# Fewer dummy matmuls, 128x32 tiles for the state weights, and a new order of steps in an attention and token-mixer kernel

## The chip, the core and the metric

The kernel runs on one core of one Trainium2 chip. The metric is the device time of one execution in microseconds. The kernel before took 88.55 us, the median of 9 runs that lay between 87.74 and 88.79.

A core has five engines that work side by side and wait for each other by semaphores: TensorE (PE in the profile; its weight loads are shown apart as PEld), VectorE (DVE), ScalarE (ACT), GpSimd (POOL) and SyncE (SP). [...] DMAs are issued here by SP, ACT and POOL.

## The reference

For each of 8 batches and 8 heads there are 512 tokens x of width 64 and 32 states of width 64. The first half reads the states by softmax attention from the tokens (`xread`) and the tokens from the states (`sread`); the second half is a token mixer on the 544 rows of both, with the heads side by side (width 512).

```python
scores  = x @ state.T / 8;        a  = softmax(scores)      # over 32 states
xread   = a @ state
scores2 = state @ x.T / 8;        a2 = softmax(scores2)     # over 512 tokens
sread   = a2 @ x
y   = concat(xread, sread)                    # (8, 544, 512), heads side by side
wq, wk  = y @ w_q, y @ w_k                    # width 64
W_tok   = wq @ wk.T / 8                      # 544 x 544
out = relu(W_tok @ y) @ w_out
```

## The kernel before

The kernel never forms the 544 x 544 matrix. For each batch it forms `wk.T @ y`, which is 64 x 512 (the tile V), and multiplies it by `wq`. It also never forms `xread`: since `xread = a @ state`, the product `xread @ w_q` is `a @ (state @ w_q)`, and `state @ w` (the "state weights", tile `sw`) is computed once for all batches.

All work is cut into named steps. One string, `ORDER`, lists them as `name.batch.mode`; the kernel walks the list and emits the instructions of each step. There is no scheduler behind it: each engine's queue is in the order of the list, and an engine that has to wait holds up all that is behind it in its queue. The pools hand out buffers in the same order. The last letter is the engine or form: `a` ScalarE, `v` VectorE, `p` POOL, `s` a DMA of SP; for TensorE `t` is one matmul of the whole 128x128 array, `c` the same work as two matmuls of 64 columns side by side (128x64 tiles), `r` a form with its own tiling.

The steps of a batch b, in the order of its data:

- `ix`: POOL issues the load of x (512 KB as bf16; POOL's DMA converts from float32). Batch 0 comes by other queues and is cast by `xc`. `iwo` loads w_out, `is` the later states.
- `xT0`, `xT1` (lines 262 to 274, by the helper of lines 165 to 174): TensorE transposes x, heads 0 to 3 and 4 to 7; `xTe` copies the result out of PSUM.
- `pt`, `exp`: scores and their exponentials, the tile E, in two halves.
- `rs`, `rinv`, `A` (lines 330 to 351): row sums of E on VectorE, their reciprocals, and on POOL the normalised tile A. `rs0.b` and `rs1.b` sum one half each, `rs.b` both halves in one instruction.
- `at`, `ate`: A transposed, and copied out (AT).
- `sums`, `srd`, `srn`, `sbd`, `srT`, `srTe`: the attention of the states to the tokens. `srd` is 32 matmuls of 128x32 tiles.
- `wq`, `wks`, `wk`, `g`, `v` and their copies `wqe`, `wke`, `ge`, `ve`: the token mixer's two factors.
- `mix`, `mixs` (64x128 tiles) with `mxe`, `mse`: the mixed rows with the relu (tile rmix).
- `fin`, `oe`, `os`: the product with w_out for 128 tokens at a time. Two such products share a PSUM tile, are copied out together (`oe`) and stored with one DMA of 512 KB (`os`). `fix` and `oc` are the same for 128 tokens alone, with a store of 256 KB issued by ScalarE (mode `a`) or SP. Mode `b` splits the copy and the store of the last piece between two engines. `fs`, `fse` are the rows of the states, four batches at a time.

At the start the states are transposed (`stt`) and copied into the tile stT by `ste` and `stf` (lines 209 to 230): the upper 64 partitions hold the heads of one half, the lower 64 those of the other, and the rest is zero, written by `zst`. `stbd` is a block form of the states that POOL builds. `sw` (lines 241 to 262) multiplies them with w_q and w_k: for two batches, four heads q and two halves r, 16 matmuls of 128 columns.

`fill` (lines 152 to 155) issues dummy matmuls on a tile of zeros, 128 x 512, into a PSUM tile that nobody reads. Eight more, on line 132, stand ahead of everything.

PSUM has two pools: psA with 2 tiles of two banks (`fill`, `sw`, `mix`, `fin`) and psB with 4 tiles of one bank (all else). The pool `tail` holds the single output pieces on their way out.

Of the kernel before, what the change touches and what calls it, by code (L numbers as in the profile page):

```python
# [13 lines left out]


ORDER = """
zst.0.p ix1.0.p stc.0.v xc1.0.a fill.1.t stt.0.c ste.0.v stbd.0.p stf.0.a xc0.0.p xc3.0.v ix2.0.p
fill.7.t xT0.0.t xc2.0.v xTe0.0.a fill.1.t xT1.0.t is.0.p stc.1.v fill.1.t stt.1.c xTe1.0.v stbd.2.p
fill.1.t pt0.0.t stf.1.v fill.1.t pt1.0.t exp0.0.a ste.1.v iwo.0.p exp1.0.a rs0.0.v fill.4.t
sums.0.t ix3.0.p rinv0.0.v wc.0.a fill.1.t xT0.1.t rs1.0.v fill.1.t srd.0.r xTe0.1.v A0.0.p fill.1.t  # L20
xT1.1.t fill.1.t sw.0.r xTe1.1.a rinv1.0.v fill.1.t pt0.1.t srn.0.v A1.0.p at0.0.t srT.0.t exp0.1.a
pt1.1.t srTe.0.v sbd.0.p swe.0.a xT0.2.t rs0.1.v at1.0.t exp1.1.a xT1.2.t xTe0.2.v stbd.1.p ate.0.a
xTe1.2.v fill.1.t stt.2.c stt.3.c rs1.1.v ste.2.a pt0.2.t stbd.6.p stf.3.v exp0.2.a fill.1.t wq.0.c
ste.3.v wks.0.c ix4.0.p stf.2.a wk.0.t rs0.2.v sw.3.r pt1.2.t wke.0.v swe.3.a stbd.3.p sw.1.r
rinv.1.v exp1.2.a g.0.t sw.2.r ge.0.v stbd.5.p swe.1.a rs1.2.v sums.2.t v.0.c wqe.0.a rinv.2.v
xT1.3.c swe.2.a A.1.p ve.0.v xT0.3.c xTe1.3.a srd.2.r xTe0.3.v mix0.0.r mix1.0.r mxe0.0.v sums.1.t
mxe1.0.a A.2.p srd.1.r at.1.t pt1.3.t srn.1.v ate.1.a fin0.0.t srn.2.v ix5.0.p xT1.4.t exp1.3.a
srT.1.t xT0.4.t xTe1.4.v srTe.1.a fin1.0.t sbd.1.p xTe0.4.a rs1.3.v pt1.4.t wq.1.c sbd.2.p exp1.4.a
wks.1.c wqe.1.v pt0.4.t oe0.0.a srT.2.t wk.1.t rs1.4.v at.2.t ix6.0.p fin2.0.t ate.2.v wke.1.a
os0.0.s exp0.4.a stbd.7.p g.1.t srTe.2.v fin3.0.t ge.1.v rs0.4.v sums.4.t stbd.4.p oe1.0.a srd.4.r  # L30
rinv.4.v v.1.c srn.4.v wq.2.c A.4.p ve.1.a os1.0.s srT.4.c wks.2.c wk.2.t srTe.4.a mixs.1.r wke.2.v
mix1.1.r wqe.2.a mix0.1.r mse.1.v xT1.5.t mxe0.1.a ix7.0.p at.4.t xTe1.5.v g.2.t xT0.5.t mxe1.1.a
ge.2.v sbd.4.p pt1.5.t xTe0.5.v v.2.c exp1.5.a fin2.1.c ve.2.v pt0.5.c rs1.5.v mixs.2.r mix1.2.r
exp0.5.a ate.4.v xT1.6.c mse.2.a sums.5.c fin3.1.c xTe1.6.a rs0.5.v rinv.5.v xT0.6.c mxe1.2.a
oe1.1.v A.5.p pt1.6.c wq.4.c srd.5.r exp1.6.a mix0.2.r srn.5.v os1.1.s fin0.1.c mxe0.2.a rs1.6.v
sbd.5.p xT0.7.c xTe0.6.v fin0.2.c xTe0.7.a wqe.4.v pt0.6.c srT.5.c at.5.c exp0.6.a xT1.7.c ate.5.v
srTe.5.a fin1.2.c xTe1.7.a rs0.6.v wq.5.c rinv.6.v wks.5.c wk.5.c wqe.5.a pt1.7.c A.6.p wke.5.v
wks.4.c sums.6.c exp1.7.a srd.6.r g.5.t oe0.2.a rs1.7.v wk.4.t pt0.3.t fin1.1.t srn.6.v exp0.3.a
os0.2.s wke.4.v sbd.6.p at.6.t oe0.1.a rs0.3.v srT.6.t g.4.t fin2.2.t ate.6.v os0.1.s fin3.2.t
ge.5.v ge.4.v srTe.6.v v.5.c oe1.2.a rinv.3.v wq.6.c ve.5.v A.3.p wks.6.c wk.6.c v.4.c os1.2.s  # L40
wke.6.a wqe.6.v mix1.5.r ve.4.a mixs.5.r mix0.5.r mxe1.5.v sums.3.t mxe0.5.a g.6.t srd.3.r mixs.4.r
ge.6.v mix0.4.r mse.5.a mix1.4.r srn.3.v mxe0.4.a v.6.c mse.4.v sbd.3.p srT.3.c pt0.7.c srTe.3.v
at.3.c mxe1.4.a ve.6.v fin2.5.c ate.3.v exp0.7.a fin3.5.c rs0.7.v wq.3.c oe1.5.a wks.3.c fin0.4.c
rinv.7.v A.7.p wqe.3.a os1.5.s mix0.6.r mixs.6.r wk.3.t mse.6.a fin1.4.t wke.3.a mxe0.6.a g.3.t
oe0.4.v at.7.t sums.7.t ate.7.a srd.7.r mix1.6.r srn.7.v os0.4.s fin2.4.c mxe1.6.v sbd.7.p srT.7.c
fin3.4.c srTe.7.a ge.3.v fin2.6.c oe1.4.v v.3.c fin3.6.c ve.3.v os1.4.s fin0.5.c oe1.6.a fin1.5.c
os1.6.s mix1.3.r oe0.5.v mixs.3.r wq.7.c mxe1.3.a wks.7.c wk.7.c mixs.0.r mse.3.v mix0.3.r os0.5.s
mse.0.a wke.7.v fin0.6.c wqe.7.a mxe0.3.a g.7.c fin1.6.c ge.7.a fin0.3.c oe0.6.v fin1.3.c os0.6.s
v.7.c oe0.3.a fin2.3.c ve.7.a fin3.3.c os0.3.s mix0.7.r oe1.3.a mixs.7.r fs.3.t mxe0.7.v mse.7.a
os1.3.s mix1.7.r fse.3.v fs.7.t mxe1.7.a fse.7.v fix1.7.t fix2.7.t oc1.7.a fix0.7.t oc2.7.a fix3.7.t  # L50
oc0.7.a oc3.7.b
"""


# [1 line left out]
def kernel(  # L56
# [20 lines left out]
    NP = H // 2  # L77
# [3 lines left out]

    const = ctx.enter_context(tc.tile_pool(name="const", bufs=1))
    work = ctx.enter_context(tc.tile_pool(name="work", bufs=4))
    tail = ctx.enter_context(tc.tile_pool(name="tail", bufs=7))
    psA = ctx.enter_context(tc.tile_pool(name="psA", bufs=2, space=bass.MemoryType.PSUM))
    psB = ctx.enter_context(tc.tile_pool(name="psB", bufs=4, space=bass.MemoryType.PSUM))

# [4 lines left out]
    stT = const.tile([128, B, 2, H, NS], BF, name="stT")  # L92
    stbd = const.tile([128, B, 2, NP, D], BF, name="stbd")
    w_f = const.tile([128, NP, 2, DH], FP, name="w_f")
    w_qk = const.tile([128, NP, 2, DH], BF, name="w_qk")
    w_o = const.tile([128, KC, DM], BF, name="w_o")
    sw = const.tile([128, B, 2, 2, DH], BF, name="sw")
# [143 lines left out]
    def sw_mm(n, p, e):  # L241
        ps = psA.tile([128, 2, 512], FP, name="sw_ps", tag="psA")
        for bb in range(2):
            for q in range(NP):
                for r in range(2):
                    nc.tensor.matmul(
                        out=ps[NS * q : NS * q + NS, r, 2 * DH * bb : 2 * DH * bb + 2 * DH],
                        lhsT=stT[64 * r : 64 * r + 64, 2 * p + bb, r, NP * r + q, :],
                        rhs=w_qk[64 * r : 64 * r + 64, q, 0:2, :],
                        start=True,  # L250
                        stop=True,
                    )
        G["sw", p] = ps
# [363 lines left out]
    def fs_ev(n, b, e):  # L617
# [7 lines left out]
        "zst": zeros, "stt": st_tr, "ste": st_ev, "stf": st_ev,  # L625
        "stbd": stbd_blk, "fill": fill, "fix": fin_mm, "os": fin_st,
        "sw": sw_mm, "swe": sw_ev, "xT": xT_mm, "xTe": xT_ev, "xs": x_dT, "as": a_dT, "pt": pt_mm, "exp": pt_exp,
        "rs": rs, "rinv": rv, "A": nrm, "at": at_mm, "ate": at_ev,
        "srd": srd, "sums": sums, "srn": srn, "sbd": sbd, "srT": srT_mm, "srTe": srT_ev,
# [38 lines left out]
```

The softmax here doesn't subtract the row's maximum and nothing guards it: scores larger than these inputs give would overflow.

## Time and profile before

| | before |
|---|---|
| median of 9 runs | 88.55 us |
| lowest, highest | 87.74, 88.79 us |
| the profiled execution | 88.63 us |
| its span in the profile | 86.9 us |
| TensorE busy | 80.4 us (93%) |
| VectorE, ScalarE, POOL busy | 52.3, 56.0, 45.1 us |
| last matmul ends | 82.8 us |
| last store landed | 85.9 us |
| output stores: 512 KB, 256 KB, 128 KB pieces | 14, 5, 2 |
| granted TensorE clock | 1.0 |

The profile is of one execution. Its span starts with the first instruction that the profile shows; 1.7 us of the measured time lie outside. Busy time of TensorE is not a measure of how near it is to its peak, since matmuls are pipelined and their ends are modelled; the starts are measured. Some records of matmuls are missing, among them a few of line 155 and 163.

### The profile page before, as it was taken

The page shows a single profiled execution, that of the slowest core. Times are in us where ns is not written, and L with a number is a line of the kernel's source. Part 1 is how long each engine was busy: PE and PEld are TensorE (multiplying, and loading weights), DVE is VectorE, ACT ScalarE, POOL GpSimd, SP SyncE. Part 2 cuts the span into 40 slices and gives each one's busy share as a digit, 9 for nine tenths or more (in the row PEclk, how much of TensorE's full clock was granted, in tenths as well). Part 3 has the DMA queues.
Part 4 walks back from the last instruction along what each step waited for, and adds up shares of the span by engine and source line. Part 5 has one row for each costly group of instructions (what it writes and reads, how often), then busy time and mean ns, then how long its engine had stood idle before and what let it go on. Part 6 is the DMA issues. An engine that isn't in the chain of part 4 may idle for free.

```text
span 86.9 us, 3553 instructions
## 1 busy us (share of the span) xinstructions
PE 80.4 (93%) x1572; PEld 53.2 (61%) x1579; DVE 52.3 (60%) x111; ACT 56.0 (64%) x83; POOL 45.1 (52%) x58
## 2 busy tenths in 40 slices
PE   4999999999999999999899999999999999999910
PEld 1336676868777688777479747866755565544400
DVE  2135993997956867887746957881688264056010
ACT  1543629989888678588597838967930592665530
POOL 7999969999999969308506735327150000000000
PEclk9999999999999999999999999999999999999999
DMA  0899999999709999993600374201461663566782
GB/s 18 284 320 188 207 188 200 193 159 140 100 6 119 154 129 307 294 169 55 245 8 0 145 315 183 104 8 57 185 234 57 274 283 134 213 270 276 292 316 82
DMA packets 15119, 15.00 MB, mean 173 GB/s; under 512 B 3712, under 2 KB 12672, under 8 KB 15104
## 3 DMA queue, kind: packets, MB, share of 16 engines
q0 software_dynamic: 9104, 4.36, 40.7%
q1 hardware_dynamic: 4880, 8.98, 27.9%
q10 hardware_dynamic: 1120, 1.44, 4.6%
q8 instruction: 12, 0.20, 0.9%
q14 instruction: 3, 0.02, 0.1%
HBM read 10.22 MB, written 8.91 MB: 220 GB/s over the span
## 4 chain that ended last, share of the span: by engine, by line
PE 76%; DMA 10%; ACT 4%; DVE 2%; POOL 2%; issue 1%; POOLq 0%
PE fin_ps L161 17%; PE fin_ps L163 11%; DMA x_bf<-in_x_dram 10%; PE fill_ps L155 6%; PE xT_ps L174 4%; PE mix_ps L541 4%; PE warm_ps L132 4%; PE at_ps L174 2%; PE srd_ps L369 2%; PE xT_ps L170 2%; POOL A L346 2%; PE pt_ps L163 2%; PE fins_ps L163 2%; PE v_ps L505 2%; PE g_ps L163 2%; PE wq_ps L433 2%
## 5 line engine op out<-in xcount | busy, mean ns | idle before, releaser
L346 POOL TENSOR_TENSOR A<-E,rinv 128x1024 bf16<-128x1024 bf16 (+1 forms) x9 | 15.4, 1716 | 12.5 <-DVE rinv L340 12.1
L161 PE MATMUL fin_ps<-w_o,rmix 128*64 128x512 bf16 x160 | 19.4, 380 | 0.0
L142 ACT COPY ost<-fin_ps 128x1024 f32<-128x1024 f32 (+2 forms) x13 | 11.2, 864 | 11.6 <-PE fin_ps L161 5.9
L148 ACT ACTIVATE rmix<-mix_ps 128x1024 bf16<-128x1024 f32 x12 | 12.1, 1024 | 2.4 <-PE mix_ps L541 2.4
L407 POOL TENSOR_TENSOR sbd<-srn,mask 128x256 bf16<-128x256 bf16 x16 | 9.4, 613 | 6.0 <-DVE srn L397 5.9
L144 DVE COPY ost<-fin_ps 128x1024 f32<-128x1024 f32 (+1 forms) x6 | 6.5, 1091 | 9.9 <-PE fin_ps L163 5.4
L161 PEld LDWEIGHTS <-rmix 128*64 128x64 bf16 x160 | 8.4, 110 | 6.2 <-issue 0.6
L332 DVE TENSOR_REDUCE rsum<-E 128x16 f32<-128x512 bf16 x16 | 10.8, 676 | 0.8 <-ACT E L317 0.6
L163 PE MATMUL fin_ps<-w_o,rmix 128*128 128x512 bf16 x44 | 11.0, 379 | 0.2
L317 ACT ACTIVATE E<-pt_ps 128x512 bf16<-128x512 f32 x16 | 9.5, 601 | 2.4 <-PE pt_ps L161 1.3
L142 ACT COPY xT<-xT_ps 128x1024 bf16<-128x1024 bf16 x7 | 7.1, 1012 | 4.3 <-PE xT_ps L174 3.1
L234 POOL TENSOR_TENSOR stbd<-st_bf,mask 128x256 bf16<-128x256 bf16 x16 | 9.3, 610 | 0.4 <-DVE st_bf L144 0.4
L144 DVE COPY xT<-xT_ps 128x1024 bf16<-128x1024 bf16 x9 | 6.2, 691 | 2.1 <-PE xT_ps L174 1.9
L155 PE MATMUL fill_ps<-zero 128*128 128x512 bf16 x21 | 7.4, 408 | 0.1
L150 DVE TENSOR_SCALAR rmix<-mix_ps 128x1024 bf16<-128x1024 f32 x4 | 4.9, 1222 | 3.4 <-PE mix_ps L541 3.4
L163 PEld LDWEIGHTS <-rmix 128*128 128x128 bf16 x48 | 4.3, 98 | 4.0 <-ACT rmix L148 0.2
L183 POOL DMA_DIRECT2D x_bf<-in_x_dram x7 | 6.6, 949 | 0.0
L174 PE MATMUL xT_ps<-ident,x_bf 128*128 128x128 bf16 x80 | 6.0, 219 | 0.2 <-ACT E L317 0.2
L174 PEld LDWEIGHTS <-x_bf 128*128 128x128 bf16 x80 | 5.1, 98 | 1.3 <-issue 0.5
L541 PE MATMUL mix_ps<-wq,V 64*128 64x256 bf16 x64 | 5.8, 272 | 0.0
L132 PE MATMUL warm_ps<-zero 128*128 128x512 bf16 x8 | 3.6, 631 | 1.2 <-DVE mask L133 1.2
L144 DVE COPY AT<-at_ps 128x1024 bf16<-128x1024 bf16 x5 | 3.4, 687 | 1.9 <-PE at_ps L170 1.7
(90 smaller groups left out, 140.2 us busy)
## 6 DMA issues: line engine op xcount, KB each, us to landing
out_dram<-ost SPq DMA_DIRECT2D x14, 512.0 KB, 2.7
x_bf<-in_x_dram POOLq DMA_DIRECT2D x7, 512.0 KB, 7.5
out_dram<-ost ACTq DMA_DIRECT2D x3, 256.0 KB, 2.1
x_f<-in_x_dram ACTq DMA_DIRECT2D x2, 256.0 KB, 4.2
x_f<-in_x_dram SPq DMA_DIRECT2D x2, 256.0 KB, 4.6
w_o<-in_moe_w_out_dram POOLq DMA_DIRECT2D x1, 512.0 KB, 8.8
out_dram<-ost SPq DMA_DIRECT2D x2, 256.0 KB, 2.4
st_bf<-in_state_dram POOLq DMA_DIRECT2D x1, 160.0 KB, 7.6
```

The source lines that it names most:

```text
L142: nc.scalar.copy(out=out, in_=in_)
L144: nc.vector.tensor_copy(out=out, in_=in_)
L148: nc.scalar.activation(out=out, in_=in_, func=AF.Relu)
L155: nc.tensor.matmul(out=ps, lhsT=zero[:, 0:128], rhs=zero, start=True, stop=True)
L161: nc.tensor.matmul(out=out[64 * h : 64 * h + 64], lhsT=lh, rhs=rhs, **kw)
L163: nc.tensor.matmul(out=out, lhsT=lhsT, rhs=rhs, **kw)
L174: nc.tensor.transpose(out=out, in_=in_, identity=ident)
L234: nc.gpsimd.tensor_tensor(out=stbd[:, b, r], in0=st_bf[:, b, r : r + 1, :].to_broadcast((128, NP, D)), in1=mask[:, :, None].to_broadcast(( ...
L317: nc.scalar.activation(out=L[b]["E"][:, r].rearrange("p c q n -> p c (q n)"), in_=L[b][f"pt{r}"], func=AF.Exp, scale=float(scale),)
L332: nc.vector.reduce_sum(out=L[b]["rsum"][:, w], in_=L[b]["E"].rearrange("p r c q n -> p (r c q) n")[:, w], axis=AX.X,)
L346: eng.tensor_tensor(out=L[b]["A"].rearrange("p r c q n -> p (r c q) n")[:, w], in0=L[b]["E"].rearrange("p r c q n -> p (r c q) n")[:, w], ...
L407: nc.gpsimd.tensor_tensor(out=L[b]["sbd"][:, r], in0=L[b]["srn"][:, r : r + 1, :].to_broadcast((128, NP, D)), in1=mask[:, :, None].to_broa ...
```

## The change

- `ORDER` is another list. It has 404 steps instead of 410; 19 dummy matmuls in `fill` instead of 23, with two fewer ahead of the first transposes (`fill.5` for `fill.7`), one fewer ahead of `sums.0` (`fill.3` for `fill.4`) and none ahead of `stt.2`.
- The row sums of batches 3 to 7 are one step each (`rs.3.v`) instead of two.
- Eight output pieces of the last batches are made and stored singly: `fix2.5`, `fix3.5`, `fix2.6`, `fix3.6` with their `oc` take the place of `fin2.5` to `fin3.6` with `oe1.5`, `os1.5`, `oe1.6`, `os1.6`; the four of batch 7 were single before. The pool `tail` has 12 buffers instead of 7.
- The matmuls of `sw` read all 128 partitions of stT and of w_qk instead of 64: their weights are 128x32 tiles instead of 64x32.
- Many steps stand elsewhere in the order, and some have another engine or form: for instance `xTe0.0` and `ate.0` go from ScalarE to VectorE, four `xT` steps go from `c` to `t`, batch 3 comes in its turn instead of late, and the loads `ix3` to `ix7` stand behind other work of POOL.

```diff
-    tail = ctx.enter_context(tc.tile_pool(name="tail", bufs=7))
+    tail = ctx.enter_context(tc.tile_pool(name="tail", bufs=12))
...
-                        lhsT=stT[64 * r : 64 * r + 64, 2 * p + bb, r, NP * r + q, :],
-                        rhs=w_qk[64 * r : 64 * r + 64, q, 0:2, :],
+                        lhsT=stT[:, 2 * p + bb, r, NP * r + q, :],
+                        rhs=w_qk[:, q, 0:2, :],
```

Of the list, the first lines, a middle stretch and the last lines (cut):

```diff
 ORDER = """
-zst.0.p ix1.0.p stc.0.v xc1.0.a fill.1.t stt.0.c ste.0.v stbd.0.p stf.0.a xc0.0.p xc3.0.v ix2.0.p
-fill.7.t xT0.0.t xc2.0.v xTe0.0.a fill.1.t xT1.0.t is.0.p stc.1.v fill.1.t stt.1.c xTe1.0.v stbd.2.p
-fill.1.t pt0.0.t stf.1.v fill.1.t pt1.0.t exp0.0.a ste.1.v iwo.0.p exp1.0.a rs0.0.v fill.4.t
-sums.0.t ix3.0.p rinv0.0.v wc.0.a fill.1.t xT0.1.t rs1.0.v fill.1.t srd.0.r xTe0.1.v A0.0.p fill.1.t
-xT1.1.t fill.1.t sw.0.r xTe1.1.a rinv1.0.v fill.1.t pt0.1.t srn.0.v A1.0.p at0.0.t srT.0.t exp0.1.a
+zst.0.p ix1.0.p stc.0.v fill.1.t stt.0.c stbd.0.p xc1.0.a stf.0.v ste.0.a xc0.0.p xc3.0.v ix2.0.p
+fill.5.t xT0.0.t xc2.0.v fill.1.t xT1.0.t xTe0.0.v is.0.p stc.1.v fill.1.t pt0.0.t xTe1.0.v stbd.1.p
+fill.1.t stt.1.c exp0.0.a stf.1.v fill.1.t pt1.0.t rs0.0.v iwo.0.p exp1.0.a rinv0.0.v fill.3.t
+sums.0.t rs1.0.v A0.0.p fill.1.t xT0.1.t wc.0.a rinv1.0.v fill.1.t srd.0.r ste.1.v fill.1.t xT1.1.t
+A1.0.p srn.0.v fill.1.t at0.0.t xTe1.1.a fill.1.t sw.0.r xTe0.1.v fill.1.t srT.0.t ix3.0.p at1.0.t
+srTe.0.v pt0.1.t swe.0.a ate.0.v xT1.2.t pt1.1.t exp0.1.a sbd.0.p xTe1.2.v wq.0.c exp1.1.a wks.0.c
+rs0.1.v stt.3.c stbd.7.p wqe.0.a wk.0.t sums.1.t ste.3.v xT0.2.t wke.0.a stf.3.v pt1.2.t stbd.3.p
+xTe0.2.v srd.1.r exp1.2.a stt.2.c srn.1.v pt0.2.t ste.2.a stbd.4.p g.0.t stf.2.v srT.1.t sw.3.r
+exp0.2.a ge.0.v sw.1.r rs1.1.v v.0.c ix4.0.p swe.1.a rinv.1.v sums.2.t ve.0.a srTe.1.v srd.2.r A.1.p
...
-oe1.1.v A.5.p pt1.6.c wq.4.c srd.5.r exp1.6.a mix0.2.r srn.5.v os1.1.s fin0.1.c mxe0.2.a rs1.6.v
-sbd.5.p xT0.7.c xTe0.6.v fin0.2.c xTe0.7.a wqe.4.v pt0.6.c srT.5.c at.5.c exp0.6.a xT1.7.c ate.5.v
+mxe1.2.v wk.3.t mse.2.a xT1.6.t wke.3.a xT0.6.t xTe1.5.a mxe0.2.v pt1.4.t fin2.1.t exp1.4.a pt1.5.t
+xTe1.6.v fin0.1.t exp1.5.a xTe0.6.v sums.4.t pt1.6.t rs.5.v g.3.t exp1.6.a fin1.1.t ge.3.a fin3.1.t
+rinv.5.v oe0.1.a rs.4.v A.5.p xT0.7.t oe1.1.a fin0.2.t os0.1.s rinv.4.v xTe0.7.v fin1.2.t os1.1.s
...
-v.7.c oe0.3.a fin2.3.c ve.7.a fin3.3.c os0.3.s mix0.7.r oe1.3.a mixs.7.r fs.3.t mxe0.7.v mse.7.a
-os1.3.s mix1.7.r fse.3.v fs.7.t mxe1.7.a fse.7.v fix1.7.t fix2.7.t oc1.7.a fix0.7.t oc2.7.a fix3.7.t
-oc0.7.a oc3.7.b
+mse.6.v mse.5.a mix1.6.r wke.7.v mxe0.6.a fix3.5.c g.7.c mxe1.6.a oc3.5.v fin0.5.c fin1.5.c ge.7.a
+wqe.7.a fin0.6.c oe0.5.a fin1.6.c os0.5.s v.7.c oe0.6.a fix2.5.c ve.7.a fix2.6.c os0.6.s oc2.5.v
+mixs.7.r mix0.7.r oc2.6.v mse.7.a mix1.7.r fix3.6.t mxe1.7.a mxe0.7.v fs.7.t oc3.6.a fix0.7.t
+fse.7.v fix3.7.t oc0.7.a fix2.7.t oc3.7.v fix1.7.t oc2.7.v oc1.7.b
```

POOL's queue, from the two lists (DMA issues in bold):

- before: zst, **ix1**, stbd.0, xc0, **ix2**, **is**, stbd.2, **iwo**, **ix3**, A0.0, A1.0, sbd.0, stbd.1, stbd.6, **ix4**, stbd.3, stbd.5, A.1, A.2, **ix5**, sbd.1, sbd.2, **ix6**, stbd.7, stbd.4, A.4, **ix7**, sbd.4, ...
- after: zst, **ix1**, stbd.0, xc0, **ix2**, **is**, stbd.1, **iwo**, A0.0, A1.0, **ix3**, sbd.0, stbd.7, stbd.3, stbd.4, **ix4**, A.1, stbd.2, **ix5**, A.2, sbd.1, sbd.2, **ix6**, A.3, sbd.3, stbd.5, **ix7**, stbd.6, A.5, ...

## The prediction

> **What bounds the kernel now.** I read the page's busy shares first, then the stretches of time, then the chain of work that ended last, and last the queue of POOL.
>
> ```profile
> span 86.9 us, 3553 instructions
> ...
> PE 80.4 (93%) x1572; PEld 53.2 (61%) x1579; DVE 52.3 (60%) x111; ACT 56.0 (64%) x83; POOL 45.1 (52%) x58
> ...
> 20.00:42.00 22.00, 21.79 (x545) 16.66 (x546) 17.16 (x36) 17.91 (x27) 17.25 (x21) 1.00 0.96 157
> 42.00:83.00 41.00, 40.28 (x738) 25.33 (x741) 22.95 (x43) 26.08 (x38) 9.85 (x10) 1.00 0.43 171
> ```
>
> The columns of the last two lines are the stretch, its length, and the busy time of PE, PEld, DVE, ACT and POOL. TensorE has no free time from 20 to 83 us; every other engine has. The chain says what lies between its steps:
>
> ```profile
> 5.56 1.89 PE fill_ps L155 x7
> 9.44 0.23 PE pt_ps L163 x8
> 14.23 0.60 ACT E L317
> 14.88 0.61 PE xT_ps L174 x8
> 17.66 0.50 ACT E L317
> 18.20 0.32 PE wk_ps L459 x8
> 18.86 0.23 PE sw_ps L246 x16
> 19.09 0.34 PE pt_ps L163 x8
> 33.31 8.87 DMA x_bf<-in_x_dram
> 42.18 0.04 issue
> 42.22 0.64 PE xT_ps L170 x16
> ```
>
> Columns: start, length, what. Three things are to be seen. The same eight pt matmuls take 0.23 us behind a fill and 0.34 behind sw: 0.11 us belongs to the change of tile shape. TensorE waits in three places: at 14.88 and 18.20 for ACT, at 42.22 for a load of x. In the single starts of the trace these waits are 0.34, 0.30 and 0.49 us, 1.13 together. And a load of x takes up to 8.87 us from issue to landing. POOL issues these loads between its other work:
>
> ```profile
> 27.50 0.94 POOL L183 DMA_DIRECT2D x_bf<-in_x_dram  x1
> 28.46 2.32 POOL L234 TENSOR_TENSOR stbd<-st_bf,mask 128x256 bf16<-128x256 bf16 x4
> 31.46 1.91 POOL L346 TENSOR_TENSOR A<-E,rinv 128x1024 bf16<-128x1024 bf16 x1 [0.68 <-DVE rinv L340]
> 33.31 0.94 POOL L183 DMA_DIRECT2D x_bf<-in_x_dram  x1
> ```
>
> So the time is the sum of TensorE's steps, the drains between them and its waits, up to its last matmul at 82.78 us; behind that stand 4.1 us of copy and store (86.9 - 82.8).
>
> **What the Trainium skill says.** "TensorEngine Tiling (Array Packing)", Key Properties: "Changing tiling mode (not just tile) drains the TensorE". The trace agrees: where the next step has another tile shape, its first matmul starts a median of 94 ns later than the columns of the last one explain (58 such places after the warm-up; 67 to 100 ns nearly everywhere), and 0 ns where the shape stays. "TensorE: Matmul & The Clock Gate", The mechanism: matmuls start in strict program order, with no reordering. In the trace the sixteen of one sw step never overtake: the first eight, on eight different tiles, start 3.4 ns apart. The same page, "Wait — 56ns, not 53.3ns?", gives 55.6 ns from start to start at 128 columns; the xT transposes (128 columns, one tile) show 56, and srd (64 columns) returns to the same tile after 29.5. "VectorE: DVE Perf Modes", the tier table, has tensor_reduce at the plain rate only, so one merged reduction costs about what two cost, less one start.
>
> **The change part by part.** Durations are from the rows of this execution (88.63 us, span 86.9; 1.73 outside the span, unchanged). The median of the nine runs is 88.55; I subtract from that.
>
> Fewer fills: 23 to 19, at 0.216 us from start to start, 0.86. Two go before the first transposes, one before sums.0, one before stt.2. The first three (0.65) stand where data is late. With two fewer, xT0.0 starts at 6.86 instead of 7.29. Then VectorE must do xTe0.0 (0.69, moved there from ACT), stc.1 (0.69) and xTe1.0 (0.69), from about 7.5 to 9.5, and pt1.0 starts near 9.55 instead of 9.73. Its exp (0.2 to drain, 0.60) ends near 10.55: sums.0 gains 0.27. The fourth fill counts in full. Together -0.5.
>
> New order: counted along TensorE's queue, the steps change tile shape 46 times instead of 58 (fills, xT, pt and the like in 128x128 stand together more often; four of the xT steps go from halves to whole). 12 x 0.094 = -1.1.
>
> State weights: 64 matmuls in four steps, as before, but of 128x32 tiles instead of 64x32. Before, the pair r=0, r=1 lay on different rows and ran side by side. Now both want the same column tile, one straight behind the other. Before, the sixteenth matmul starts 90 ns after the first (trace). After: each second one of a pair waits 55.6, the next pair starts 3.5 later, so 8 x 55.6 + 7 x 3.5 = 469 ns. 4 x 0.379 = +1.5. No row shows this order of tiles. Bounds: if the four columns overlapped as freely as in srd, the step would stay at its old length or gain 0; if each of the sixteen waited for the one before, 15 x 55.6 = 834, +3.0. I take 1.5, because start order is strict in every row.
>
> Waits: the 1.13 us of the three waits go, as the new order puts other work there (xTe and ate of the front go from ACT, at 1.01 each, to DVE, at 0.69). New ones: stt.3 behind VectorE's srTe, ate and xTe1.2 (a PSUM bank), sw.1 behind ACT's ste.2 (0.79), which starts only after exp1.2: I estimate 0.15 each, +0.3.
>
> Loads of x: POOL's queue decides. x3 is now issued behind A0.0 and A1.0 (1.04 each) instead of before them: near 12.9 instead of 10.15. It still queues behind w_o, which landed at 18.13, with x3 2.7 later at 20.79; so I expect it at 20.8 to 21.3, and xT1.3 wants it near 21.5. Between x3 and x4 stand sbd and three stbd (4.6), so x4 goes out near 18.6 (before 17.3), wanted near 29. x6 goes out behind A.2 and two sbd, near 29.5 (before 27.5), x7 near 34.7 (before 33.3). x6 landed after 7.5, x7 after 8.9 us: at 37.0 to 38.4 and 41.6 to 43.6. TensorE wants them near 37.4 and, 5.5 us of steps later, near 42.8. Nothing, or about 0.7 us: half of that, +0.35.
>
> Merged row sums: five pairs of 0.676 become five of about 1.2 (1,024 elements at the rate of the 512 row, less one start): VectorE saves 0.7 in all. It has 18 us free after 42; worth 0. A half's exp no longer starts its sum, so rinv comes up to 0.6 later; A of these batches has over 1 us before at wants it. If that cover is gone, up to 0.6.
>
> Single stores: two pairs (oe, 1.01 each on ACT) become four pieces (oc, 0.69 on VectorE, 0.59 on ACT), each with its own store: three more stores on SP, one fewer on ACT (0.35 us of issue each). The queues are free there, and the last piece is split and stored as before: 0. Were SP late at the end, 0.3. Engine changes of other steps: 0 for the same reason.
>
> Sum: -0.5 - 1.1 + 1.5 - 1.13 + 0.3 + 0.35 = -0.6 us: span 86.3, time 88.55 - 0.6 = 88.0.
>
> **The rivals.** (a) Loads late: x6 and x7 take 8.9 us or more, because the stores of batch 0 now leave during x5's and x6's loads. +0.7 to the sum, 88.6 to 88.7: no change. For it: x7 took 8.87 with stores beside it; against: x5 took 6.8.
> (b) Slower: x3 takes 10.64 us from issue, as it did before, instead of being queued behind w_o only. Then it lands at 23.5, TensorE waits 2.0 us at xT1.3, and the later load waits (0.35) vanish: -0.6 + 2.0 - 0.35, so 89.6. It makes the kernel slower than before from a wait of 0.95 us on, which is about 9.6 us of latency (x3 at 22.5). For it: that is the measured latency of this very transfer; against: most of it was waiting for w_o.
> (c) The sw matmuls run wholly one by one: +1.5 more, 89.5.
> (d) The sw steps cost nothing extra, since the array overlaps the pairs in some way: 86.5. For it only that nothing shows this order; against it the strict starts.
> A change that doesn't do what it says isn't open: the queue of the built program holds 19 fills, 64 sw matmuls of 128x32 and 11 row sums.
>
> **How the numbers follow.** A measurement of this kernel tells about 0.5% (0.44 us) from nothing. The forecast, 87.4 to 88.4, gets 0.48, (a) 0.22, (b) 0.12, (c) 0.08, (d) 0.10. Faster by over 0.5% is below 88.11: two thirds of the forecast and a little more, 0.38, and (d): 0.48. Slower, above 88.99: (b), (c) and a tail of (a), 0.23. The rest, 0.29, is the same. The range 87.0 to 89.5 leaves out (d) and the ends of (b) and (c). The likeliest case's own range is 87.4 to 88.4.
>
> **What would show it.** The sw steps: 0.5 to 0.6 us each in order of time instead of 0.23, starts in pairs 56 ns apart, and sw_ps busy 2.4 to 2.8 us instead of 1.22. TensorE's last matmul near 82.2. No wait of TensorE at 14 to 19 us over 0.2. The first xT transpose at 6.9, but sums.0 only 0.3 earlier than 10.8. Loads x6 and x7 landing within 8 us, no wait over 0.4 at their transposes. It is wrong if TensorE stands before xT1.3 for the load issued behind A1.0, or before xT1.6; if a drain costs less where steps were put together; or if the row sums let rinv come so late that at waits.

## The result and the profile after

The changed kernel took 89.01 us (median), the kernel before 88.29 us on the same chip. The ratio is 1.0096, 95% interval 1.0073 to 1.0118: slower by about 1%. The forecast had been 88.0 us, 0.6 us faster than the 88.55 us of the first nine runs. The profiled executions lie closer together than the medians: 88.85 us (span 87.1) against 88.63 us (span 86.9). The first is 0.16 us below the median of its kernel, the second 0.34 us above. So the traces below explain 0.2 us of the difference line by line; the other 0.5 us is what these two executions lie off their medians, and no line of them can place it.

The page of the changed kernel, its first lines:

```profile
span 87.1 us, 3478 instructions
...
PE 79.6 (91%) x1541; PEld 53.3 (61%) x1547; DVE 53.5 (61%) x109; ACT 52.8 (61%) x82; POOL 45.0 (52%) x58
```

The busy time by stretches, changed kernel (stretch, length, then PE, PEld, DVE, ACT, POOL, the granted clock, the DMA share, GB/s):

```profile
20.00:42.00 22.00, 20.45 (x442) 15.69 (x445) 17.23 (x31) 16.59 (x27) 15.29 (x18) 1.00 0.92 146
42.00:83.00 41.00, 40.73 (x780) 26.14 (x781) 24.09 (x45) 26.13 (x38) 12.22 (x12) 1.00 0.45 177
```

From 20 to 42 us TensorE now has 1.55 us without work, where it had 0.21 before; after 42 it has 0.27, where it had 0.72. So the new idle time lies between 20 and 42. The chain of work that ended last names the places (start, length, what):

```profile
18.60 0.80 ACT stT L141
19.42 0.57 DVE stT L143
...
25.57 1.90 POOL A L345
27.47 2.24 POOL sbd L406 x4
29.71 9.13 DMA x_bf<-in_x_dram
38.90 1.07 PE xT_ps L173 x16
```

The large entry is the load of x6: 9.13 us from its issue to its landing, behind POOL's A.2 and sbd.1 and sbd.2. The timeline of TensorE shows two smaller stops, with what ended the idle time in brackets:

```profile
20.04 0.30 PE L245 MATMUL sw_ps<-w_qk,stT 128*32 128x128 bf16 x7 [0.36 <-DVE stT L143]
...
21.11 0.24 PE L368 MATMUL srd_ps<-x_bf,E 128*32 128x64 bf16 x8
21.61 0.36 PE L368 MATMUL srd_ps<-x_bf,E 128*32 128x64 bf16 x24 [0.26 <-issue]
```

The first is sw.1, which waits for the copy stf.2 on VectorE; that copy itself waited 0.75 us for ste.2 on ScalarE. The second stands in the middle of a step and has no releaser; I come back to it.

Matmul ends are modelled, so I worked out TensorE's times from start to start. A stop is the time by which a start comes later than the columns of the matmul before it and a change of tile shape (94 ns) explain. It is therefore a little longer than the idle time in brackets: 1.31 us at xT1.6, for instance, where the timeline has 1.15.

| Term | predicted, us | changed minus before in the traces, us |
|---|---|---|
| four fewer fills | -0.5 | -0.86, and 0.30 of new short stops at 8.3, 10.5 and 10.9 |
| order: 46 changes of tile shape instead of 58 | -1.1 | -1.13 |
| state weights | +1.5 | 4 x 0.107 = +0.43 |
| old waits gone | -1.13 | -1.26 (two small ones more) |
| new waits | +0.3 | sw.1 0.52, inside srd.2 0.42, at 15.9 and 17.1 together 0.28, others 0.15: +1.37 |
| loads of x | +0.35 | xT1.6 waits for x6: +1.31 |
| sum | -0.6 | +0.16 |

TensorE's last matmul starts 0.15 us later than before (82.54 against 82.39), so the right column accounts for the traces, though not for the medians. Behind the last matmul nothing changed: in both, 4.1 us of copy and store.

### The profile page after: what moved, and what is told of

Its sections match the earlier page's. It is cut to its first block, busy times and chain, and to the rows that moved or that the text cites. A ratio compares the mean times of both kernels' runs of the same rounds, so it can differ in the third digit from the quotient of the medians.

```text
span 87.1 us, 3478 instructions
## 1 busy us (share of the span) xinstructions
PE 79.6 (91%) x1541; PEld 53.3 (61%) x1547; DVE 53.5 (61%) x109; ACT 52.8 (61%) x82; POOL 45.0 (52%) x58
## 4 chain that ended last, share of the span: by engine, by line
PE 73%; DMA 10%; DVE 5%; POOL 5%; ACT 1%; issue 1%; POOLq 0%
PE fin_ps L160 16%; PE fin_ps L162 12%; DMA x_bf<-in_x_dram 10%; PE xT_ps L173 6%; PE fill_ps L154 6%; PE warm_ps L131 4%; PE mix_ps L540 3%; PE srd_ps L368 3%; POOL sbd L406 3%; PE pt_ps L162 2%; POOL A L345 2%; PE stT_ps L214 2%; PE v_ps L504 2%; PE at_ps L169 2%; PE wq_ps L432 2%; PE v_ps L513 2%
## 5 line engine op out<-in xcount | busy, mean ns | idle before, releaser
L141 ACT COPY ost<-fin_ps 128x1024 f32<-128x1024 f32 (+2 forms) x15 | 13.6, 916 | 11.2 <-PE fin_ps L160 3.5
L160 PE MATMUL fin_ps<-w_o,rmix 128*64 128x512 bf16 x144 | 17.3, 380 | 0.0
L162 PE MATMUL fin_ps<-w_o,rmix 128*128 128x512 bf16 x51 | 13.1, 379 | 0.3
L331 DVE TENSOR_REDUCE rsum<-E 128x16 f32<-128x512 bf16 (+1 forms) x11 | 10.0, 912 | 1.5 <-ACT E L316 1.5
L149 DVE TENSOR_SCALAR rmix<-mix_ps 128x1024 bf16<-128x1024 f32 x8 | 9.6, 1219 | 0.5 <-PE mix_ps L540 0.3
L173 PE MATMUL xT_ps<-ident,x_bf 128*128 128x128 bf16 x112 | 8.6, 219 | 1.1 <-DMA x_bf<-in_x_dram 1.1
L147 ACT ACTIVATE rmix<-mix_ps 128x1024 bf16<-128x1024 f32 x8 | 8.0, 1029 | 0.4 <-PE mix_ps L540 0.4
L143 DVE COPY ost<-fin_ps 128x512 f32<-128x512 f32 (+1 forms) x6 | 3.9, 646 | 6.7 <-PE fin_ps L160 5.3
L141 ACT COPY xT<-xT_ps 128x1024 bf16<-128x1024 bf16 x4 | 4.0, 1011 | 1.2 <-PE xT_ps L173 1.2
L162 PE MATMUL pt_ps<-stT,xT 128*128 128x64 bf16 x96 | 4.8, 193 | 0.0
```

What stands on the lines that cost most here:

```text
L141: nc.scalar.copy(out=out, in_=in_)
L143: nc.vector.tensor_copy(out=out, in_=in_)
L149: nc.vector.tensor_scalar(out=out, in0=in_, scalar1=0.0, scalar2=None, op0=ALU.max)
L160: nc.tensor.matmul(out=out[64 * h : 64 * h + 64], lhsT=lh, rhs=rhs, **kw)
L162: nc.tensor.matmul(out=out, lhsT=lhsT, rhs=rhs, **kw)
L173: nc.tensor.transpose(out=out, in_=in_, identity=ident)
```

## The experiments

Two theories stood at first. *Store collision:* the two stores of batch 0 leave at 27.7 and 30.7 us, and share the DMA engines with the load of x6. *Late issue:* x6 goes out 2.2 us later than before, and that alone is the loss.

**The load of x6 issued earlier.** One token of the list is moved, so that POOL issues it ahead of sbd.1 and sbd.2.

```diff
-A.2.p swe.2.v ... rinv.3.v ix6.0.p xT0.4.t
+A.2.p ix6.0.p swe.2.v ... rinv.3.v xT0.4.t
```

> The changed kernel with one step moved: POOL issues the load of x6 straight behind A.2 instead of behind A.2, sbd.1 and sbd.2, so about 2.3 us earlier. Theory: TensorE's wait of 1.31 us at the transposes of batch 6 is what makes the changed kernel slower, and it comes from the late place in POOL's queue: the wait falls under 0.3 us and the time by 0.8 to 1.3 us, to about the time of the kernel before or below it. Rival (stores alone): the load takes as long as it likes while the stores of batch 0 flow; issued at 27.4 it then takes 11 us instead of 9.1, and the time stays within 0.3 us of the changed kernel.

Measured: 0.9985 (0.9960 to 1.0009). That is 0.6 us better than the next run (1.0054, same session, the changed kernel in effect) and level with the kernel before. The load left 2.5 us sooner, at 27.17, and was no shorter for it (9.56 us; 10.75 and 8.82 in two later runs with the same place). The wait for it was gone from xT1.6, but TensorE stood 1.39 us inside that same step with nothing named:

```profile
37.33 0.67 PE L173 MATMUL xT_ps<-ident,x_bf 128*128 128x128 bf16 x9
39.38 0.55 PE L173 MATMUL xT_ps<-ident,x_bf 128*128 128x128 bf16 x7 [1.39 <-issue]
```

This profiled execution took 88.89 us, against a median of 88.23, so a typical one probably stops for less. The late issue is part of the loss, then, but not what makes the load long.

**The stores later in the list.**

```diff
-... os0.0.s ... os1.0.s ...
+... xT1.6.t os0.0.s os1.0.s ...
```

> The changed kernel with the two stores of batch 0 (512 KB each) issued behind the transpose xT1.6 instead of at 27.7 and 30.7 us. Theory (late place in the queue and stores both): x6 is still issued near 29.7, but takes about 7.5 us instead of 9.1, lands near 37.2, and the wait of 1.31 us falls under 0.3; the time falls by about 1 us unless x7 or a later wait takes it back. Rival (place in the queue alone): x6 takes 9 us all the same, and nothing changes within 0.3 us.

Measured: 1.0054 (1.0032 to 1.0075). This run tells nothing of the stores: SP has nothing ahead of them in its queue, so a later place in the list moved nothing, and they left at 27.68 and 30.73 as before. It is the changed kernel a second time, and shows how far the same instructions differ between sessions: 0.4%.

**The four fills put back** (23 instead of 19, at three places of the changed order).

```diff
-fill.5.t xT0.0.t ... fill.3.t ... exp1.2.a stt.2.c
+fill.7.t xT0.0.t ... fill.4.t ... exp1.2.a fill.1.t stt.2.c
```

> The changed kernel with the four dummy matmuls put back (fill.7, fill.4, and one ahead of stt.2: 23 in all). The sum of the prediction says +0.5 us for them, counted singly +0.86. Theory: whatever TensorE saves ahead of 37 us it gives back at the wait for x6, so +0.0 to +0.3 us only, with the wait at batch 6 shorter by 0.5 or more. If the stall of 0.42 us inside srd.2 belongs to the fetch of TensorE's instructions, it sits 8 instructions earlier in the step (before the fifth matmul of srd.2 instead of before the ninth) or is gone; if it belongs to data, it stays before the ninth.

Measured: 1.0121 (1.0077 to 1.0166), against 1.0054 for the run above in the same session. That is 0.0067 or 0.6 us slower, outside the 0.0 to 0.3 that was expected. But it is not the price of four fills. In the traces TensorE is 0.17 us later with the fills when it goes on at sw.1 (20.27 against 20.10); then the stop inside srd.2 is missing, and the step ahead of xT1.6, wk.3, starts earlier with the fills than without (37.20 against 37.34). What differs is the load of x6, which takes 9.42 us in place of 8.93 and lands at 39.20 in place of 38.64:

```profile
39.24 1.07 PE L173 MATMUL xT_ps<-ident,x_bf 128*128 128x128 bf16 x16 [1.64 <-DMA x_bf<-in_x_dram]
```

In the run above the same line starts at 38.69 with 0.94 in its bracket. So this run doesn't price the fills. That the stop inside srd.2 is gone was one of the two outcomes expected of a cause that goes by the count of instructions.

**The old slices of the state weights on top of the early load.**

```diff
-lhsT=stT[:, 2 * p + bb, r, NP * r + q, :],
-rhs=w_qk[:, q, 0:2, :],
+lhsT=stT[64 * r : 64 * r + 64, 2 * p + bb, r, NP * r + q, :],
+rhs=w_qk[64 * r : 64 * r + 64, q, 0:2, :],
```

> The kernel of the run with x6 issued earlier, with the matmuls of sw back on 64 partitions (64x32 tiles). The prediction priced the 128x32 form at +1.5 us; the trace of the changed kernel has the sixteen starts of a step over 197 ns instead of 90, which is +0.43 for the four steps. By the prediction this run is 1.5 us faster than the one with x6 issued earlier and 128x32 tiles; by the trace 0.2 to 0.4 us faster, or level where a later wait takes it up.

Measured: 0.9968 (0.9938 to 0.9998) against 0.9985 with the new slices: 0.15 us, inside the intervals. The +1.5 us of the prediction lies far outside them.

**The stores of batch 0 really late.** Both are issued by ScalarE, behind exp1.4, at 38.9 and 39.3 us.

```diff
-        nc.sync.dma_start(out=dst_x[b, :, 2 * p : 2 * p + 2, :], in_=L[b]["ost", p])
+        eng = nc.scalar if e == "a" else nc.sync
+        eng.dma_start(out=dst_x[b, :, 2 * p : 2 * p + 2, :], in_=L[b]["ost", p])
...
-... os0.0.s ... os1.0.s ... exp1.4.a
+... exp1.4.a os0.0.a os1.0.a
```

> The changed kernel with one edit: the two 512 KB stores of batch 0 are issued from ScalarE's queue behind exp1.4, at about 40 us, instead of from SyncE's at 27.7 and 30.7 us. The load of x6 keeps its place (issued at 29.7 us). Theory 'the stores stretch the load': x6 then flies about as long as x5 (6.4 us), lands near 36.2 us, transpose xT1.6 finds it at 37.6 us, the wait of 1.31 us is gone, and the ratio to the kernel before falls from 1.0096 to about 0.996 to 1.000. Rival 'the load is as long without them' (seven of the loads took 5.8 to 9.1 us): x6 lands after 38.2 us, over 0.6 us of the wait stay, and the ratio stays above 1.004. Third theory, 'instruction fetch': the wait for x6 covers a second limit, the arrival of TensorE's next 256 instructions at about 39.4 us (a 16 KB packet from 36.7 to 37.6 us and 1.4 us more); if that packet is not stretched by the stores, the gain is cut; without the stores the packet itself should start by about 34 us.

Measured: 0.9889 (0.9834 to 0.9943), 87.41 us. Two tokens turn a loss of 1% into a gain of 1.1%, more than the 0.996 to 1.000 expected. TensorE's last matmul starts at 81.10 in place of 82.54; 1.31 us of that is the wait at xT1.6. The DMA queues of the changed kernel during the flight of x6 (29.71 to 38.85 us): q0 carries POOL's loads, q1 the stores of SP; packets, MB, and the time of the packets as a share of all 16 DMA engines. The last line has the median flight of x6 and x7, both issued in this stretch:

```profile
q0 software_dynamic: 1375, 0.69, 67.3%
q1 hardware_dynamic: 282, 1.02, 29.0%
...
x_bf<-in_x_dram POOLq DMA_DIRECT2D x2, 512.0 KB, 8.5
```

The same view with late stores, for the flight from 29.81 to 35.65 us:

```profile
q0 software_dynamic: 1066, 0.54, 72.1%
...
x_bf<-in_x_dram POOLq DMA_DIRECT2D x2, 512.0 KB, 5.8
```

The megabyte of q1 is gone, and the load of x6 takes 5.84 us in place of 9.13. The Trainium skill says in "DMA: Bandwidth & Descriptors", Queues, rings and completion order, that each DMA engine goes round between the queues that have work, a packet at a time, and under "Issuing engines are not separate DMA queues" that all issuers end on the same engines. The trace of the changed kernel agrees: from 34 to 36 us packets of both queues run side by side (0.17 MB of the load, 0.44 MB of the store). TensorE's timeline with late stores:

```profile
37.23 0.41 PE L162 MATMUL wk_ps<-sw,AT 128*128 128x64 bf16 x8
37.47 1.06 PE L173 MATMUL xT_ps<-ident,x_bf 128*128 128x128 bf16 x16
```

xT1.6 now follows wk.3 with no bracket: no wait and no stop.

**Both at once: early load and late stores** (the first and the last edit above).

> Both edits: the load of x6 issued directly behind the weights A of batch 2, as in the run with the early load, and the two stores of batch 0 issued from ScalarE's queue at about 40 us. In the run with the early load alone, TensorE stood for 1.39 us at its 1472nd instruction with no wait named, 1.50 us after the end of a 16 KB instruction packet that had started at 36.96 us. Theory 'instruction fetch stretched by the stores': without the stores that packet starts by about 34 us, the stall at the 1472nd instruction is below 0.2 us, and the ratio is 0.007 to 0.015 below that of the early load alone (0.9985), so 0.984 to 0.992. Rival 'the packet is not the cause of the stall': the packet moves earlier and the stall stays at over 1 us, or the packet stays where it was; the ratio is then within 0.003 of 0.9985.

Measured: 0.9896 (0.9848 to 0.9943). That is 0.009 better than the early load alone, as expected, and no better than the late stores alone: x6 landed at 33.39 with nobody wanting it until 37. *Late issue* falls: once the stores are away, x6's place in POOL's queue is worth nothing.

**Which of the two stores.** One of them is moved, the other stays on SP.

```diff
-... os0.0.s ... exp1.4.a                    (first run: only this one)
+... exp1.4.a os0.0.a
-... os1.0.s ... exp1.4.a                    (second run: only this one)
+... exp1.4.a os1.0.a
```

> The changed kernel with only the first of the two stores of batch 0 (27.7 us) moved to ScalarE's queue at about 39 us; the second stays at about 30.7 us. Both moved gave 0.989, none moved 1.005 to 1.010. Theory 'bytes in flight': one store of 512 KB less takes about half of the stretch away; x6 lands 7 to 8 us after its issue at 29.7, near 37.2, the wait at xT1.6 is below 0.3 us, but the instruction packet after 33 us still starts late; ratio 0.992 to 1.000. Rival 'the store issued during the load's flight counts, the one ahead of it does not': x6 is as late as with both (over 8.5 us), ratio above 1.003.

> The changed kernel with only the second of the two stores (30.7 us) moved to ScalarE's queue at about 39 us; the first stays at 27.7 us and has its packets from 29 to 33 us. Theory 'bytes in flight': as with the other one alone, x6 lands 7 to 8 us after its issue, ratio 0.992 to 1.000. Rival 'the store issued during the load's flight counts': x6 takes about 6 us as with both moved, its packets follow those of the first store, and the ratio is 0.987 to 0.991.

Measured: with the second store left in place 1.0023 (0.9986 to 1.0059), with the first left in place 0.9927 (0.9902 to 0.9952). Landings by the loads' own semaphores:

| Kernel | x6 issued, landed, flight, us | store os0.0 | store os1.0 | TensorE at xT1.6 |
|---|---|---|---|---|
| changed | 29.71, 38.85, 9.13 | 27.67 to 33.34 | 30.73 to 37.09 | waits 1.31 |
| second store stays | 29.46, 38.41, 8.95 | late | 30.47 to 36.99 | waits 1.13 |
| first store stays | 29.79, 36.09, 6.30 | 27.66 to 32.75 | late | no wait |
| both late | 29.81, 35.65, 5.84 | late | late | no wait |

TensorE's timeline with the second store in place has the wait:

```profile
38.46 1.07 PE L173 MATMUL xT_ps<-ident,x_bf 128*128 128x128 bf16 x16 [0.97 <-DMA x_bf<-in_x_dram]
```

and with the first in place not:

```profile
37.57 1.06 PE L173 MATMUL xT_ps<-ident,x_bf 128*128 128x128 bf16 x16
```

The second store does it; half the bytes is not half the harm. Both runs have one store on ScalarE, so the change of queue alone is not what helps. The landings are clear; the ratios are less so. 1.0023 and 0.9927 lie just outside the ranges expected if only the store issued during the flight counts, and 0.9927 lies just inside that of bytes in flight. So the first store may cost something as well, 0.3 us by the ratios; the interval overlaps that of both late.

The packets tell part of the reason. With both in place, the first store's run from 29 to 32 us, before most of x6's, and the second's from 34 to 37, through the middle of them. But x6 is behind before that. From 31 to 34 us, in the changed kernel:

```profile
q0 software_dynamic: 373, 0.19, 69.3%
q1 hardware_dynamic: 23, 0.06, 5.7%
```

and with the first store alone in place:

```profile
q0 software_dynamic: 652, 0.33, 93.2%
q1 hardware_dynamic: 20, 0.06, 5.0%
```

The bytes of stores are the same (the tail of the first), yet x6 has moved 0.19 MB in place of 0.33 (0.17 and 0.28 in two more profiles with the second store but hardly a packet of it yet, 0.33 to 0.37 in four with both stores late). The second store, issued at 30.73, slows the load before its own packets show. Packets that alternate are therefore not the whole mechanism, and the rest is open.

**Late stores in the kernel before.**

```diff
-... os0.0.s ... os1.0.s ... xTe0.7.a
+... xTe0.7.a os0.0.a os1.0.a
```

> The kernel before with one edit: its two stores of batch 0 (issued at 28.9 and 31.9 us) are issued from ScalarE's queue behind xTe0.7, at about 43 us. Theory 'the same collision costs the kernel before': its load of x7, 8.87 us long, takes about 6 us without the stores, the wait of 0.49 us at 42.2 us goes, ratio 0.993 to 0.996. Then the changed kernel with late stores (0.989) is faster than the old one with late stores by only about 0.5%: so much is the rest of the change worth. Rival 'the collision is a child of the new order alone': ratio 0.998 to 1.001.

Measured: 0.9990 (0.9957 to 1.0024). The load of x7 took 5.78 us in place of 8.87 and its wait of 0.49 us is gone from the trace, whose last matmul starts 0.68 us earlier; the medians show nothing of it. The two profiled executions come from opposite ends: 88.63 us is above the median of the kernel before, 87.90 us below that of this one (88.31). And the wait is not in every execution: in the profile of the kernel before with new state weights (below), x7 took 7.55 us with both stores in place, and nobody waited. This fits the ratio, but two traces don't prove it. By the ratios, then, the edit is worth 1.5 to 1.8 us after the change (1.0054 or 1.0096 to 0.9889) and nothing measurable before it.

**The stop without a name.** With the early load and sw.1 behind srd.2, the wait at sw.1 should go:

```diff
-exp0.2.a ge.0.v sw.1.r ... swe.1.a ... srd.2.r A.1.p ... swe.3.a
+exp0.2.a ge.0.v ... srd.2.r sw.1.r A.1.p ... swe.1.a swe.3.a
```

> The changed kernel with two edits: the early load of x6, and the state-weight product sw.1 put behind srd.2 with its eviction later, so that it no longer stands at 20.0 us for the copy stf.2 on VectorE (0.52 us), itself late by 0.75 us for ste.2 on ScalarE. Theory 'the wait at sw.1 costs what the trace shows': ratio 0.005 to 0.006 below the early load alone (0.9985), so about 0.993. Rival 'instruction fetch takes the gain': TensorE comes 0.5 us sooner to its 704th instruction, whose packet ends at 20.2 us and is usable at 21.6 us; the stall there grows from 0.42 to about 0.9 us, and the ratio stays at 0.998 to 1.000.

Measured: 0.9997 (0.9971 to 1.0024), no better than the early load alone (0.9985). The 0.52 us at sw.1 went, and came back in pieces: v.0 stands 0.47 us (for ScalarE's exp, mostly) and 0.21 in the place that sw.1 used to fill, mix 0.25, and srd.2, now earlier, has 0.16 at its old place. The rival was right in outcome, but only this last piece is what it named. In xT1.6, in the same run, the stop of the early load shows again:

```profile
37.56 0.67 PE L173 MATMUL xT_ps<-ident,x_bf 128*128 128x128 bf16 x9
38.40 0.55 PE L173 MATMUL xT_ps<-ident,x_bf 128*128 128x128 bf16 x7 [0.18 <-issue]
```

It stands behind nine of sixteen transposes of one tile, for which all data is there. Counted in the records of TensorE's queue, matmuls and weight loads, the stops without a releaser are at instructions 448, 704 and 1472: 192 and a multiple of 256. The DMA queue named "instruction" moves packets of 16 KB. The Trainium skill ("Vector Engine (DVE) Microarchitecture Reference", Instruction fetch and dispatch) has 64 bytes to an instruction; it says so on the page of VectorE, and if TensorE's are as long, a packet holds 256. To test it, the changed kernel got eight instructions more at its start, where TensorE waits anyway:

```diff
-zst.0.p ix1.0.p stc.0.v fill.1.t
+zst.0.p ix1.0.p stc.0.v fill.1.x
...
+        for w in range(4 if e == "x" else 0):
+            nc.tensor.matmul(out=ps[:, 0:64], lhsT=zero[:, 0:128], rhs=zero[:, 0:64], start=True, stop=True)
```

> The changed kernel with four small products of zeros more in the first fill at about 4.6 us, where TensorE waits for data anyway; they are eight instructions. In the changed kernel TensorE stands 0.42 us inside the products srd.2 at 21.6 us, in front of the eleventh times 64th instruction of its queue, behind 8 of the 32 products with x; no wait is named. Theory 'arrival of the next 256 instructions': the stall stays at the same count from the start of the queue, and so comes eight instructions earlier in the program, behind 4 of the 32 products instead of 8. Rival 'something in srd.2 itself (its data, its bank, the weights)': it stays behind the eighth product.

Measured: 89.21 us (one execution). The stop in srd.2, which the test was for, did not come: the packet started at 18.58 us in place of 19.32. But the one in xT1.6 did:

```profile
37.87 0.45 PE L175 MATMUL xT_ps<-ident,x_bf 128*128 128x128 bf16 x5
39.55 0.77 PE L175 MATMUL xT_ps<-ident,x_bf 128*128 128x128 bf16 x11 [1.23 <-issue]
```

Behind five in place of nine: four matmuls and four weight loads earlier, the eight instructions. The stop belongs to a count from the start of the queue and not to the step. In all seventeen profiles there are 187 such block starts; none comes sooner than 1.26 us after the end of its packet, and at those of them where TensorE stops over 0.14 us with no wait named, 1.26 to 1.55 us have passed. In the changed kernel the packet for instruction 704 ended at 20.22 and the block began at 21.61, 1.39 later. That an instruction packet is behind the stop is thus well supported; that nothing else in its timing plays in was not tried.

It also fits the early load. The profile counts packets of instructions on the same 16 DMA engines as loads and stores. The one for instruction 1472 starts 3.0 to 4.5 us after TensorE has begun the block before, in all eight profiles of the changed order with the second store in place (3.76 in the changed kernel itself), and 0.2 to 2.6 us after it in all six with that store late. So with the second store two things come late, the load and the instructions. Take away the wait for the load alone, and TensorE stops later in the same step: 1.39 us in the execution shown above, 0.18 in the one shown here.

**The state weights by themselves.** The new slices in the kernel before:

```diff
-lhsT=stT[64 * r : 64 * r + 64, 2 * p + bb, r, NP * r + q, :],
-rhs=w_qk[64 * r : 64 * r + 64, q, 0:2, :],
+lhsT=stT[:, 2 * p + bb, r, NP * r + q, :],
+rhs=w_qk[:, q, 0:2, :],
```

> The kernel before with one edit alone: the products of the state weights in the new form (128 rows by 32 columns). The prediction had this at +1.5 us (4 x 0.379), from the thought that two neighbours on the same column group run one after the other: ratio about 1.017. The trace of the changed kernel has 16 starts over 0.197 us instead of 0.090 us: +0.43 us, ratio about 1.005, less if the mode switches on both sides that stay (64x32 had other neighbours) are cheaper: not below 1.000. Rival 'it costs nothing' (hidden under other waits): 0.998 to 1.001.

Measured: 1.0031 (1.0003 to 1.0058), +0.27 us. The old slices in the changed kernel with late stores:

> The changed kernel with the late stores of batch 0 and with the state weights in their old form of 64 rows by 32 columns. With the new form and late stores the ratio was 0.9889. Theory 'the form costs what its starts show' (4 x 0.107 = 0.43 us): 0.984. Rival 'it is hidden' (0 to 0.15 us, as the pair of runs with the early load had it): 0.987 to 0.989. The prediction's +1.5 us would give 0.972.

Measured: 0.9897 (0.9852 to 0.9943), 87.28 us: no difference to the new slices (0.9889). Intervals of half a per cent to each side leave room for the 0.43 us of the trace, but not for 1.5. And the two loops exchanged, so that no neighbours share a column group:

```diff
-            for q in range(NP):
-                for r in range(2):
+            for r in range(2):
+                for q in range(NP):
```

> The changed kernel with late stores and, in the state weights, the two loops exchanged: first the four column groups of r=0, then those of r=1, so that no two neighbours in the queue share a column group. If same-group neighbours are what spaces the starts (four starts 6.5 ns apart, then about 56 ns to the next four), the exchange changes the grouping: four different groups start together and the step takes 3 x 56 + 20 = 0.19 us, as now, if the array already worked on several of one group, and no less. If the starts are held by something else that goes by fours, such as the number of weight loads in flight, the pattern is the same, 0.19 to 0.21 us over sixteen starts. If neighbours on one group cost extra, the step gets shorter than 0.15 us.

Measured: 87.14 us (one execution). The starts of the sixteen matmuls of one step, in ns from the first:

```
before, 64x32        0   4   7  10  14  17  20  24  67  70  73  76  80  84  86  90
changed, 128x32      0   6  13  20  66  72  80  86 122 128 136 141 178 184 191 197
loops exchanged      0   3   7  10  67  69  73  76 122 125 129 132 178 181 185 187
```

Eight start per round with 64 rows; four with 128 rows, in either order of the loops. A round is 56 to 67 ns. So the form costs two rounds more a step, 0.107 us, and the order inside costs next to nothing (197 against 187 ns).

**The row sums split again**, in the changed kernel with late stores:

```diff
-rs.3.v        (and rs.4 to rs.7)
+rs0.3.v rs1.3.v
```

> The changed kernel with both stores late (0.989) and its five merged row sums split again into halves, one behind the other at the same place: five of 1.20 us become ten of 0.67 us, 0.7 us more of VectorE in all. The prediction's step: 0, VectorE is no bound: ratio 0.987 to 0.991. Rival: VectorE's evictions stand ahead of TensorE at these places, so that each pair's 0.14 us goes on the path: up to 0.7 us, ratio 0.993 to 0.997.

Measured: 0.9915 (0.9888 to 0.9941), 87.31 us, against 0.9889 and 87.41 us merged. No difference can be told. Had merging cost 0.6 us, as the prediction feared, the split form would be faster by 0.007, and the intervals exclude that; that splitting costs 0.7 us they just fail to exclude. Nothing speaks against the 0.

## Why the prediction was wrong, point by point

**Loads of x.** This is the step that failed. "x7 took 8.87 with stores beside it; against: x5 took 6.8": the mechanism of rival (a) was named, and given 0.22. But the step took the flights of 7.5 and 8.9 us as a spread, each end half likely, and carried it over to the new order. There x6 has two cases: 5.5 to 6.3 us in the six profiles without the second store, and 8.2 to 10.8 in the eight with it (the two longest, 9.56 and 10.75, are early loads in executions well above their medians). It landed at 38.85, where TensorE wanted it at 37.6: +1.31, not +0.35. A stand of TensorE "before xT1.6" was among the prediction's own signs of being wrong. It was x6 alone; x7 was in time (42.78). The rival's price of +0.7 was about half of what x6 alone cost.

By times of issue alone, the trace of before did not tell which case x6 would be. There os0.0 was issued 1.4 us behind ix6, much as os1.0 is in the new order, and x6 took 7.49; both were issued ahead of ix7, and x7 took 8.87. Their packets ran from 33 to 37 us, behind most of x6's and ahead of most of x7's. What the prediction left out is the question where a store's packets would fall in x6's flight.

**New waits.** "sw.1 behind ACT's ste.2": right place, but priced at 0.15, and 0.52 in the trace. Removing that wait bought nothing, because other waits then came into the open. The stop inside srd.2 (0.42), and the one in xT1.6 that the wait for x6 covers, had no place in the sum at all: TensorE's own instructions arrive by DMA, and here the packets came late.

**State weights.** The mechanism was wrong. "Both now want the same column tile, one straight behind the other" is so, but the one does not wait for the other's end: two on one column group start 6.5 ns apart. The Trainium skill's strict order of starts ("TensorE: Matmul & The Clock Gate", The mechanism) is not the same as waiting for the neighbour's end; whether it holds inside a step can't be read here, since the rows don't tell its sixteen matmuls apart. The trace gives +0.43, the run by itself +0.27; too dear by 1.1 to 1.2 us. Rival (c) is excluded, (d) nearly right.

**Right, as far as shown.** Fills: -0.86 and 0.30 of new stops in the traces, so -0.56 against -0.5; the run with the fills put back doesn't price them. Changes of tile shape: 12 x 0.094, the trace gives the same, though the order had no run of its own. The three removed waits did go. Row sums 0. Single stores 0, by the trace only: 4.1 us behind the last matmul in both. Rival (b) did not come: x3 landed at 20.33, sooner than the 20.8 of the forecast, and nobody waited for it. Two readings of lines were loose, without weight in the sum: TensorE's "no free time from 20 to 83 us" is 0.9 us in the lines above those words, and the longest load was not the 8.87 us of x7 but the 10.64 of x3.

Errors of opposite sign partly hid each other: -1.1 for the state weights, +1.0 for x6, +1.1 for the other new waits. With the stores out of the way, the changed kernel takes 0.989 of the kernel before, 1.0 us less; the prediction's sum without its term for loads is -0.9. That this fits is in part luck, since the other two errors still cancel in it.

## What to carry to other kernels

A load's flight time has to be taken by its company: list what else is under way in its flight, on any queue, and look where the packets fall, not only when they are issued. If two durations stand for two kinds of company, a middle value stands for neither. An output that nobody waits for can be stored later, on a queue that has other work ahead of it; moving its place in a list does nothing if its queue is empty. Here that paid in the new order and not in the old one. Before a slower run is taken as the price of what was put back, see in its trace where the time went: with the four fills it went into a longer load. When a wait that was removed comes back as a stop with no releaser, look at the instruction packets before the step itself.

## What the runs showed of the hardware that I had not expected

TensorE's instructions come in blocks of 256, by packets of 16 KB over the shared DMA engines; a block started 1.26 us after its packet's end at the earliest. Where the second store ran beside the load of x6, the packet began 3.0 to 4.5 us after the block before, and TensorE stood up to 1.39 us with no wait named (1.23 in another execution); without it, 0.2 to 2.6 us and no stop.

POOL's 512 KB load of x6 took 5.5 to 6.3 us by itself or behind a store of 512 KB, and 8.2 to 10.8 us with such a store issued about 1 us after it (3 us with the early load); part of the delay came before the store's packets. In the kernel before, x7 took 8.87 and 7.55 us with the stores there and 5.78 without. Matmuls of 128 columns started four per 56 to 67 ns as 128x32 tiles, whichever tiles were neighbours, and eight per 67 ns as 64x32 tiles in the one order that ran.
